# Preparing two tiles ahead of weight conversions, early loads of float64 units, and zero fills behind the fifth tile

## The chip, the cores and the metric

The kernel runs on one core of one Trainium2 chip. The metric is the device time of one execution in microseconds; the figure of a kernel is the median over its runs. The trace is one further execution, taken by the hardware profiler. PE is TensorE (matmuls), PEld its weight loads, DVE VectorE, ACT ScalarE, POOL GpSimd, SP SyncE, which here only starts transfers. SPq, ACTq and POOLq are DMA starts by those engines.

## The reference

Three stages follow each other, cut here to what is computed:

```
for t in range(768):                                   # recurrent attention, 4 x 8 heads of 48
    state = alpha[:, :, t, :, None] * state + outer(k[:, :, t], v[:, :, t])
    y[:, :, t] = q[:, :, t] @ state
x = y as (3072 tokens, 384)

logits = x @ w_gate + modality_bias[modality_id]       # 8 experts, the best one is taken
e_idx = argmax(logits);  gate_w = softmax(logits)[e_idx]
for e in range(8):
    out[mask] = gate_w * (relu(x[mask] @ w1[e]) @ w2[e])   # w1: 384 x 1024, w2: 1024 x 384

h = out @ w_in                                         # float64 weights, 384 x 2048
result = (h * sigmoid(h)) @ w_out                      # float64 weights, 2048 x 384
```

The tokens' experts are known only when the attention has run, so which rows a tile of 128 tokens holds and which expert's weights it needs are values that the kernel computes and reads back into registers.

## The kernel before

**Order of the work.** `attention` handles 24 steps of 128 positions and sorts the tokens' rows by expert: each step's rows are scattered by POOL to a table XS in DRAM, at a place that their expert and rank give. After 16 steps the most frequent expert is known, and its first 256 rows are taken as two early tiles, whose two expert products run in float32 at the end of `attention` (`early`). After step 24 a chain of small DVE operations (`table`) writes `tabi`, the list of the remaining tiles: expert, first row, and whether the expert's weights must be loaded anew. `main` then works through these tiles (slots 0, 1, 2, ...; `slot32` for the first three, in float32, `slot` for the others, in pairs of float16 numbers) and, in between, through chunks of 256 finished tokens of the last stage: `into` is the product with `w_in`, `outof` that with `w_out`. The beginning is slot 0, slot 1, `into` of chunk 0, slot 2, `outof` of chunk 0. With the early tiles counted, slot 2 is the fifth tile.

**A slot.** `fetch` (SP) reads 128 rows of XS to `xr`; ACT scales them by the gate's weight; PE transposes them to `u_p` in PSUM; ACT copies these to `xg`, the operand of the first product. `weights` (SP) loads an expert's four pieces of 768 KB to `raw` 0 to 3 (0 and 1 hold w1, 2 and 3 w2). The first product (`h_p`) needs `raw` 0 and 1 and `xg`, the second (`yT_p`) `raw` 2 and 3. At the end `keep_ids` stores the rows' token numbers with a matmul to `id_p` and a DVE copy to `idrow`.

**The float64 weights.** They come as 32 units of 384 words for each partition (0 to 15 of `w_in`, 16 to 31 of `w_out`). `unit_load` starts the transfer of 384 KB to one of two buffers `uraw`; `unit_conv` makes a float32 word in `wf` out of it on DVE (one TENSOR_SCALAR, two SCALAR_TENSOR_TENSOR), ACT rounds that to float16 (`wih`, `woh`), and DVE computes the rest (`wil`, `wol`). A buffer's next load stands behind its conversion. Units 0 to 8 (`CONV_A = 9`) are converted in `attention`'s plan, the others in `main`'s.

**Who sets the order.** Every operation is entered in a `Plan` with its engine, an estimated cost, what it reads and writes, and a priority (the smallest first). `Plan.run` lets an engine that falls free take the ready operation of the smallest priority, by estimated times, and writes out each engine's instructions in that order. On the chip each engine then works in this order, and waits on semaphores where an operand isn't there. `attention` and `main` are two plans: all of the first plan's instructions of an engine precede the second's. A plan knows nothing of what the other has left unfinished. In `main` PE is taken to be free from 2.0 us on (`PE0`). A key `seq` makes operations of one name follow each other in the order in which they are entered.

**Rows of XS.** Writes of rows are declared independent of each other (`apart`); a fetch waits for all writes of rows that have been written out before it (`behind`), and these include the eight zero fills of `zeros`, which write 128 empty rows behind each expert's last row.

Of the kernel before, what the change touches and what calls it, by code (L numbers as in the profile page):

```python
# [12 lines left out]
I32 = mybir.dt.int32  # L13
# [7 lines left out]
P = 128  # L21
B, H, S, D = 4, 8, 768, 48
NC = S // P
NSTEP = B * NC
NP = H // 2
DM = H * D
# [6 lines left out]
E = 8  # L33
# [171 lines left out]
class Kernel:  # L205
    def __init__(self, ctx, tc, qka, al0, v, vT, mod, gate, mbias, w1, w2, wi, wo, out):
        self.ctx, self.tc, self.nc = ctx, tc, tc.nc
        nc = tc.nc
        self.PE, self.ACT, self.DVE, self.POOL, self.SP = nc.tensor, nc.scalar, nc.vector, nc.gpsimd, nc.sync
        self.qka, self.al0, self.v, self.vT = qka, al0, v, vT  # L210
        self.mod, self.gate, self.mbias = mod, gate, mbias
        self.w1, self.w2, self.wi, self.wo, self.out = w1, w2, wi, wo, out

        self.rows = []
        const = self.pool(ctx, "const")
        keep = self.pool(ctx, "keep")
        dram = self.pool(ctx, "dram", space=DRAM)
        self.XS = dram.tile([E * CAP + P, ROW], F32, name="XS")

        self.wih = keep.tile([P, NF2, KD, P], F16, name="wih")  # L220
        self.wil = keep.tile([P, NF2, KD, P], F16, name="wil")
        self.raw = [keep.tile([P, 4 * DM], F32, name=f"raw{j}") for j in range(4)]
        self.uraw = [keep.tile([P, 2 * UNIT], I32, name=f"uraw{j}") for j in range(2)]
        self.wf = [keep.tile([P, UNIT], I32, name=f"wf{j}") for j in range(2)]
        self.yT0 = [keep.tile([P, KD, P * EARLY], F16, name=f"yT0{s}") for s in "hl"]
        self.xr = [keep.tile([P, ROW], F32, name=f"xr{j}") for j in range(3)]
        self.idc = [keep.tile([P, 1], I32, name=f"idc{j}") for j in range(4)]

        self.ident = const.tile([P, P], F32, name="ident")
        self.ident16 = const.tile([P, P], F16, name="ident16")  # L230
        self.w128 = const.tile([P, 1], F16, name="w128")
        self.ones16 = const.tile([P, P], F16, name="ones16")
        self.before16 = const.tile([P, P], F16, name="before16")
        self.rev = const.tile([P, E], F32, name="rev")
        self.ebase = const.tile([P, E], F32, name="ebase")
        self.pid = const.tile([P, 1], F32, name="pid")
        self.tabi = const.tile([P, 5], I32, name="tabi")
        self.cum = const.tile([P, E], F16, name="cum")
        self.star = const.tile([P, E], F32, name="star")
        self.endf = const.tile([P, E], F32, name="endf")  # L240
        self.endi = const.tile([P, E], I32, name="endi")
        self.pick = const.tile([P, 1 + EARLY], I32, name="pick")
# [27 lines left out]
        self.DVE.tensor_tensor(out=out, in0=in0, in1=in1, op=op)  # L270


    def unit_load(self, pl, u, prio, after=()):
        raw = self.uraw[u % 2]
        src = self.wi if u < NUNIT else self.wo
        c = UNIT * (u % NUNIT)
        pl.op("ACT", 0.4, lambda: self.ACT.dma_start(out=raw, in_=src[:, c:c + UNIT].bitcast(I32)),
              r=after, w=[("uraw", u % 2)], prio=prio, dma=1.1)

    def unit_conv(self, pl, u, prio):  # L280
        raw = self.uraw[u % 2].rearrange("p (a b) -> p a b", b=2)
        hw, lw = raw[:, :, 1], raw[:, :, 0]
        w = self.wf[u % 2]
        wf = w.bitcast(F32)
        hi, lo = (self.wih, self.wil) if u < NUNIT else (self.woh, self.wol)
        fl = (lambda t: t.rearrange("p a b c -> p (a b c)")) if u < NUNIT else flat
        c = UNIT * (u % NUNIT)
        hv, lv = fl(hi)[:, c:c + UNIT], fl(lo)[:, c:c + UNIT]
        s = 16.0 if u < NUNIT else 32.0
        kr, kw, ko = ("uraw", u % 2), ("wf", u % 2), ("w2nd", u)  # L290
        pl.op("DVE", c_dve(UNIT, fast=True), lambda: self.DVE.tensor_scalar(
            out=w, in0=hw, scalar1=3, scalar2=0x3FFFFFFF,
            op0=ALU.logical_shift_left, op1=ALU.bitwise_and), r=[kr], w=[kw], prio=prio)
        pl.op("DVE", c_dve(UNIT), lambda: self.stt(w, hw, -0x40000000, w, ALU.bitwise_and, ALU.bitwise_or),
              r=[kr], w=[kw], prio=prio)
        pl.op("DVE", c_dve(UNIT), lambda: self.stt(w, lw, 29, w, ALU.logical_shift_right, ALU.bitwise_or),
              r=[kr], w=[kw], prio=prio)
        pl.op("ACT", c_act(UNIT), lambda: self.act(hv, wf, scale=s), r=[kw], w=[ko], prio=prio)
        pl.op("DVE", c_dve(UNIT), lambda: self.stt(lv, wf, s, hv, ALU.mult, ALU.subtract), r=[kw], w=[ko], prio=prio)
# [14 lines left out]
    def attention(self, ctx):  # L314
# [372 lines left out]
        for i in range(NSTEP):  # L687
            if i + 2 < NSTEP:
                prep(i + 2)
            if i + 4 < NSTEP:  # L690
                load(i + 4)
            chunk(i)
            if i == EARLY_AT:
                for a in range(EARLY):
                    self.fetch(pl, None, i + 1.5, a)
                self.weights(pl, None, PICK + 2)
        for u in range(CONV_A):
            self.unit_conv(pl, u, 100 + u)
            if u + 2 < 2 * NUNIT:
                self.unit_load(pl, u + 2, 100 + u)  # L700


        def view(key, off, n, shape, dt=F32):
# [12 lines left out]
                      ("y_p", d) if d < 2 else "A0") for d in range(KD)]  # L716
        vt = float(NSTEP) + 2
        self.early(pl, vt)
        self.weights(pl, 0, NSTEP + 1)
        self.fetch(pl, 0, NSTEP + 2)  # L720
        self.fetch(pl, 1, NSTEP + 2)
        pl.run()

    def choose_early(self, pl, a1, tot_p, pr):
# [24 lines left out]

        pl.op("DVE", 0.2, ends, r=["tot_p", "dc"], w=["ends"], prio=pr + 2)  # L750

    def zeros(self, pl, prio):

        def fill(e):
            row = self.POOL.value_load(self.endi[0:1, e:e + 1], min_val=e * CAP, max_val=e * CAP + NT)
            self.apart(self.POOL.dma_start(out=self.XS[ds(row, P), :], in_=self.XS[E * CAP:E * CAP + P, :]))

        for e in range(E):
            pl.op("POOL", 1.1, lambda e=e: fill(e), r=["zero"], w=[("XS", NSTEP + e)], prio=prio + 0.1 * e, dma=0.6)

    def table(self, pl, a1, tot_p, pr):

# [79 lines left out]
    def fetch(self, pl, t, prio, early=None):  # L842
        n = self.ring_of(t, early)
        xr, kxr = self.xr[n], ("xr", n)

        def get():
            row = self.val(self.SP, t, 1, 0, E * CAP) if t is not None else self.SP.value_load(
                self.pick[0:1, 1 + early:2 + early], min_val=0, max_val=E * CAP)
            self.behind(self.SP.dma_start(out=xr, in_=self.XS[ds(row, P), :]))

        pl.op("SP", 1.1, get, r=["tab" if t is not None else "pick"] + [
            ("XS", i) for i in (range(PICK) if t is None else range(NSTEP) if t < FULL else range(NSTEP + E + 1))], w=[kxr], prio=prio, dma=0.6)

    def weights(self, pl, t, prio):
        SP = self.SP
# [35 lines left out]
    def main(self, ctx):  # L891
# [25 lines left out]
        for w in ORDER:  # L917
            if w == "i":
                vt = self.chunk_in(pl, 0, vt)
            elif w == "o":  # L920
                vt = self.chunk_out(pl, 0, vt)
            else:
                t += 1
                vt = self.step(pl, t, vt)
            if t == 1 and w == "s":
                self.zeros(pl, vt)
                for u in range(CONV_A, 2 * NUNIT):
                    pr = CV0 + CV1 * (u - NUNIT)
                    self.unit_conv(pl, u, pr)
                    if u + 2 < 2 * NUNIT:  # L930
                        self.unit_load(pl, u + 2, pr)
        for c in range(1, NCHUNK - 2):
            assert all(self.spot(u)[0] > 2 * c + 1 for u in range(t + 1, NSLOT))
            vt = self.chunk_in(pl, c, vt)
# [43 lines left out]
    def keep_ids(self, pl, t, xr, kxr, kyp, vt):  # L978
# [1 line left out]
        lo, hi = self.spot(t)  # L980
        pl.op("PE", 0.07, lambda: self.mm(self.id_p[0:2, :P], xr.bitcast(F16)[:, 2 * DM:2 * DM + 2], self.ident16, True, True),
              r=[kxr, kyp], w=["id_p"], prio=vt + 7)
        pl.op("DVE", 0.3, lambda: self.DVE.tensor_copy(out=self.idrow[:, ds(self.place(self.DVE, t), P)], in_=self.id_p[0:2, :P]),
              r=["id_p"], w=[("TC", b) for b in range(lo, hi + 1)], prio=vt + 9)

    def slot32(self, pl, t, vt):

        act, mm = self.act, self.mm
        n = self.ring_of(t, None)
        xr, kxr = self.xr[n], ("xr", n)  # L990
        xT, kxT = self.xg[t % 2].bitcast(F32).rearrange("p (a b) -> p a b", b=P), ("xg", t % 2)
        tp, ktp = self.u_p[t % 2][:, :DM].rearrange("p (a b) -> p a b", b=P), ("u_p", t % 2)
        y_p, kyp = self.y_p[0].rearrange("p (a b) -> p a b", b=P), ("yT_p", 0)
        pl.op("ACT", c_act(DM) + 0.05, lambda: act(xr[:, :DM], xr[:, :DM], scale=xr[:, DM + 1:DM + 2]), w=[kxr], prio=vt - GV)

        def transp():
            for k in range(KD):
                self.PE.transpose(out=tp[:, k], in_=xr[:, P * k:P * k + P], identity=self.ident)

        pl.op("PE", 0.34, transp, r=[kxr], w=[ktp], prio=vt - GV, work=0.3)  # L1000
        pl.op("ACT", c_act(DM, True) + 0.05, lambda: act(xT, tp), r=[ktp], w=[kxT], prio=vt - GV)
        for half in range(2):
            w = self.raw[half].rearrange("p (k f) -> p k f", k=KD)
            hp, khp = self.h_p[half].rearrange("p (a b) -> p a b", b=P), ("h_p", half)
# [275 lines left out]
```

## Time and profile before

| | us |
|---|---|
| median of 3 runs | 776.24 (775.47 to 777.59) |
| profiled execution, its own time | 776.01 |
| its span in the trace | 774.2 |
| PE busy | 748.4 |
| DVE busy | 514.5 |
| ACT busy | 397.7 |

The profiled execution's own time is 1.8 us more than its span: what lies around the span isn't in the trace. Busy time is that of instructions at work; a DMA start counts on no engine. Matmuls are pipelined, so their durations overlap, and a stretch is read from start to start. In a timeline the columns are start, duration (of a whole run of like instructions, "x" tells how many), engine, line, operation, output and inputs, and in brackets the engine's idle time before it with what ended that.

### The profile page before, as it was taken

What the parts mean: (1) busy time and instruction counts of PE and PEld (TensorE: products, weight loads), DVE (VectorE), ACT (ScalarE), POOL (GpSimd) and SP (SyncE); (2) the same over time, 40 slices, a digit from 0 to 9 for tenths busy, and PEclk for the clock granted to TensorE, in tenths of its full rate; (3) what the DMA queues carried; (4) which work ended last, traced back from release to release, by engine and by line L of the source; (5) the groups of instructions that cost most, each with busy time, mean ns of one, the idle gap of its engine ahead of it and who ended that gap; (6) DMA issues with size and microseconds to landing.
All of it is one profiled execution on the core that took longest, in us unless ns stands there. A gap on an engine that the chain in (4) does not pass through costs nothing. (4 is left out here: it accounts for less than half of the span.)

```text
span 774.2 us, 18772 instructions
## 1 busy us (share of the span) xinstructions
PE 748.4 (97%) x7751; PEld 628.3 (81%) x7751; DVE 514.5 (66%) x847; ACT 397.7 (51%) x659; POOL 113.6 (15%) x152
## 2 busy tenths in 40 slices
PE   8999999984999999999999999999999999999996
PEld 4999898874988879879799698798896987977683
DVE  6999999955699946728477477397473883723250
ACT  4776757622356536636366375376462861613140
POOL 3345747602000101010000000000100000000000
PEclk9999999995999999999999999999999999999999
DMA  8876869386545111000034120110100553000000
GB/s 291 287 249 219 281 217 381 120 298 191 155 119 135 36 29 43 23 23 21 22 95 132 23 43 22 31 33 23 43 12 12 162 124 128 12 2 24 1 22 20
DMA packets 42027, 79.39 MB, mean 103 GB/s; under 512 B 19792, under 2 KB 29648, under 8 KB 41808
## 3 DMA queue, kind: packets, MB, share of 16 engines
q1 hardware_dynamic: 34000, 54.27, 22.7%
q10 hardware_dynamic: 4608, 12.58, 5.6%
q0 software_dynamic: 3328, 11.28, 3.9%
q8 instruction: 62, 1.02, 0.5%
q14 instruction: 29, 0.24, 0.1%
HBM read 124.12 MB, written 11.48 MB: 175 GB/s over the span
## 5 line engine op out<-in xcount | busy, mean ns | idle before, releaser
L264 PEld LDWEIGHTS <-pch 128*128 128x128 f16 x1920 | 149.2, 98 | 2.3
L267 DVE SCALAR_TENSOR_TENSOR pcl<-raw,pch 128x1536 f16<-128x1536 f32 x80 | 138.6, 1752 | 16.0 <-ACT pch L261 16.0
L264 PE MATMUL u_p<-yTh,wih 128*128 128x256 f16 x528 | 144.0, 273 | 1.1 <-PEq L949 1.1
L264 PE MATMUL u_p<-yTh,wil 128*128 128x256 f16 x528 | 143.9, 273 | 0.0
L264 PE MATMUL u_p<-yTl,wih 128*128 128x256 f16 x528 | 143.9, 273 | 0.0
L264 PE MATMUL o_p<-woh,gh 128*128 128x384 f16 x384 | 125.3, 326 | 0.0
L264 PE MATMUL o_p<-wol,gh 128*128 128x384 f16 x384 | 125.2, 326 | 0.0
L264 PE MATMUL o_p<-woh,gl 128*128 128x384 f16 x384 | 125.2, 326 | 0.0
L264 PEld LDWEIGHTS <-wih 128*128 128x128 f16 x1152 | 111.1, 98 | 15.1 <-issue 1.4
L261 ACT ACTIVATE pch<-raw 128x1536 f16<-128x1536 f32 x80 | 117.6, 1478 | 1.8 <-PE yT_p L264 1.8
L264 PEld LDWEIGHTS <-gh 128*128 128x128 f16 x768 | 73.8, 98 | 47.7
L1200 POOL DMA_INDIRECT out_dram<-osb,idc x24 | 27.0, 1127 | 551.2 <-DVE osb L1197 439.5
L264 PEld LDWEIGHTS <-pcl 128*128 128x128 f16 x960 | 93.9, 98 | 0.0
L267 DVE SCALAR_TENSOR_TENSOR gl<-g,gh 128x512 f16<-128x512 f32 x96 | 65.8, 689 | 33.2 <-ACT gh L261 32.9
L261 ACT ACTIVATE gh<-g 128x512 f16<-128x512 f32 x96 | 60.1, 629 | 48.7 <-DVE g L270 48.0
L264 PE MATMUL h_p<-xT,pch 128*128 128x128 f16 x960 | 84.4, 219 | 0.0
L264 PE MATMUL yT_p<-h,pch 128*128 128x128 f16 x960 | 83.8, 219 | 0.0
L264 PE MATMUL h_p<-xT,pcl 128*128 128x128 f16 x480 | 82.3, 219 | 0.0
L264 PE MATMUL yT_p<-h,pcl 128*128 128x128 f16 x480 | 82.0, 219 | 0.0
L1197 DVE TENSOR_SCALAR osb<-o_p 128x384 f32<-128x384 f32 x12 | 6.7, 558 | 111.7 <-PE o_p L264 111.7
L270 DVE TENSOR_TENSOR g<-u_p,sg 128x512 f32<-128x512 f32 x96 | 65.4, 685 | 16.7 <-ACT sg L261 16.3
L261 ACT ACTIVATE osb<-o_p 128x384 f32<-128x384 f32 x12 | 5.9, 490 | 136.2 <-PE o_p L264 136.2
(181 smaller groups left out, 1162.6 us busy)
## 6 DMA issues: line engine op xcount, KB each, us to landing
raw<-in_w_dram SPq DMA_DIRECT2D x94, 768.0 KB
reg<-in_qka_dram SPq DMA_DIRECT2D x23, 768.0 KB
uraw<-in_wi_dram ACTq DMA_DIRECT2D x16, 384.0 KB
uraw<-in_wo_dram ACTq DMA_DIRECT2D x16, 384.0 KB
v<-in_v_dram SPq DMA_DIRECT2D x24, 224.0 KB
xr<-XS SPq DMA_DIRECT2D x25, 200.0 KB
vT<-in_vT_dram SPq DMA_DIRECT2D x24, 192.0 KB
XS<-XS POOLq DMA_DIRECT2D x8, 200.0 KB, 3.2
```

What stands on the lines that cost most here:

```text
L261: self.ACT.activation(out=out, in_=in_, func=func, **k)
L264: self.PE.matmul(out=out, lhsT=lhsT, rhs=rhs, start=first, stop=last, skip_group_check=True)
L267: self.DVE.scalar_tensor_tensor(out=out, in0=in0, scalar=scalar, in1=in1, op0=op0, op1=op1)
L270: self.DVE.tensor_tensor(out=out, in0=in0, in1=in1, op=op)
L1197: lambda osb=osb, o_p=o_p: self.DVE.tensor_scalar(out=osb, in0=o_p, scalar1=1.0 / 65536, scalar2=None, op0=ALU.mult)),
L1200: pl.op("POOL", 1.04, lambda idc=idc, osb=osb: self.POOL.indirect_dma_start(out=self.out[:, :], out_offset=IOA(ap=idc[:, :], axis=0), in_= ...
```

## The change

Four edits. The scaling, transposing and copying of slots 0 and 1 get priority 30 below the slot's due time, where it was 3 (`g`). The fetches of slots 0 and 1 are entered ahead of slot 0's weights, with a priority one lower, and join the sequence `raw` of the weights, so that SP starts fetch 0, fetch 1, then `raw` 2, 3, 0, 1. The loads of units 4 to 8 go to five places of `reg`, the memory of the attention's inputs of steps 22 and 23 and of their decay values, in place of the two buffers; these loads and those of units 9 and 10 (to the two buffers) are started by SP at priorities 23.4 to 24.0, where ACT started them behind conversions. And `zeros` is entered behind slot 2 in place of slot 1, with a dependency on slot 2's copy to `idrow`. No arithmetic changes.

```diff
+    def unit_at(self, u):
+        n = u - 2 if 4 <= u < CONV_A else u % 2
+        return self.uraw[n], ("uraw", n)
+
     def unit_load(self, pl, u, prio, after=()):
-        raw = self.uraw[u % 2]
+        raw, kr = self.unit_at(u)
+        name, eng = ("SP", self.SP) if 4 <= u < CONV_A + 2 else ("ACT", self.ACT)
...
-        pl.op("ACT", 0.4, lambda: self.ACT.dma_start(out=raw, in_=src[:, c:c + UNIT].bitcast(I32)),
-              r=after, w=[("uraw", u % 2)], prio=prio, dma=1.1)
+        pl.op(name, 0.4, lambda: eng.dma_start(out=raw, in_=src[:, c:c + UNIT].bitcast(I32)),
+              r=after, w=[kr], prio=prio, dma=1.1)
...
+        for n in range(2, CONV_A - 2):
+            at = 22 + 6 * (n - 2)
+            self.uraw.append(part(at, 6, [6 * P], I32))
+            pl.spans["uraw", n] = [("r", at + b) for b in range(6)]
         for u in range(CONV_A):
             self.unit_conv(pl, u, 100 + u)
-            if u + 2 < 2 * NUNIT:
+            if u + 2 < 4:
                 self.unit_load(pl, u + 2, 100 + u)
+            for v in range(4, CONV_A + 2) if u == 3 else ():
+                self.unit_load(pl, v, NSTEP - 1 + 0.1 * v)
...
         self.early(pl, vt)
+        self.fetch(pl, 0, NSTEP + 1)
+        self.fetch(pl, 1, NSTEP + 1)
         self.weights(pl, 0, NSTEP + 1)
-        self.fetch(pl, 0, NSTEP + 2)
-        self.fetch(pl, 1, NSTEP + 2)
...
-    def zeros(self, pl, prio):
+    def zeros(self, pl, t, prio):
...
+            made = self.POOL.dma_start(out=self.XS[ds(row, P), :], in_=self.XS[E * CAP:E * CAP + P, :])
+            self.tc.add_manual_dep(made.ins, self.kept[t].ins.name, ...)
+            self.apart(made)
...
-            pl.op("POOL", 1.1, lambda e=e: fill(e), r=["zero"], w=[("XS", NSTEP + e)], ...)
+            pl.op("POOL", 1.1, lambda e=e: fill(e), r=[("TC", EARLY + t)], w=[("XS", NSTEP + e)], ...)
...
             ("XS", i) for i in ...], w=[kxr], prio=prio, dma=0.6,
+              seq="raw" if t in (0, 1) else None)
...
             if t == 1 and w == "s":
-                self.zeros(pl, vt)
                 for u in range(CONV_A, 2 * NUNIT):
...
+        self.zeros(pl, t, vt)
         for c in range(1, NCHUNK - 2):
...
     def slot32(self, pl, t, vt):
+        g = GV if t > 1 else 30
...
-        pl.op("ACT", c_act(DM) + 0.05, lambda: act(xr[:, :DM], ...), w=[kxr], prio=vt - GV)
+        pl.op("ACT", c_act(DM) + 0.05, lambda: act(xr[:, :DM], ...), w=[kxr], prio=vt - g)
...
-        pl.op("PE", 0.34, transp, r=[kxr], w=[ktp], prio=vt - GV, work=0.3)
-        pl.op("ACT", c_act(DM, True) + 0.05, lambda: act(xT, tp), r=[ktp], w=[kxT], prio=vt - GV)
+        pl.op("PE", 0.34, transp, r=[kxr], w=[ktp], prio=vt - g, work=0.3)
+        pl.op("ACT", c_act(DM, True) + 0.05, lambda: act(xT, tp), r=[ktp], w=[kxT], prio=vt - g)
```

## Rows read from the trace of the kernel before

**Rows 1.** The page: busy time of the engines over the span.
```profile
PE 748.4 (97%) x7751; PEld 628.3 (81%) x7751; DVE 514.5 (66%) x847; ACT 397.7 (51%) x659; POOL 113.6 (15%) x152
```
**Rows 2.** Windows of 5 us: busy times, granted clock, DMA share, GB/s.
```profile
165.00:170.00 5.00, 5.00 (x25) 4.41 (x24) 3.05 (x7) 0.91 (x2) 0.00 (x0) 1.00 1.02 416
170.00:175.00 5.00, 1.41 (x7) 0.90 (x5) 2.69 (x7) 0.80 (x2) 0.21 (x1) 0.90 0.70 249
```
**Rows 3.** Timeline of PE at the seam between the two plans.
```profile
167.79 3.62 PE L264 MATMUL A_p<-reg,eraw 128*128 128x256 f32 x16
178.42 1.54 PE L998 MATMUL u_p<-ident,xr 128*128 128x128 f32 x6 [7.01 <-DVE wil L267]
185.86 8.09 PE L264 MATMUL h_p<-xg,raw 128*128 128x128 f32 x48 [5.90 <-ACT xg L261]
...
199.38 5.62 PE L264 MATMUL h_p<-xg,raw 128*128 128x128 f32 x48
```
**Rows 4.** Timeline of ACT in the same stretch.
```profile
171.45 0.39 ACT L261 ACTIVATE yT0h<-A_p 128x256 f16<-128x256 f32 x1 [2.60 <-PE A_p L264]
...
177.31 0.52 ACT L261 ACTIVATE wih<-wf 128x384 f16<-128x384 f32 x1 [1.28 <-DVE wf L267]
...
177.75 1.12 ACT L261 ACTIVATE xr<-xr 128x384 f32<-128x384 f32 x2
183.86 0.52 ACT L261 ACTIVATE wih<-wf 128x384 f16<-128x384 f32 x1 [4.99 <-DVE wf L267]
...
184.39 0.49 ACTq L277 DMA_DIRECT2D uraw<-in_wi_dram  x1
185.31 0.87 ACT L261 ACTIVATE xg<-u_p 128x384 f32<-128x384 f32 x2 [0.46 <-DMA XS<-XS]
```
**Rows 5.** Timeline of DVE in the same stretch.
```profile
157.83 0.17 DVE L748 CAST endi<-endf 128x8 int32<-128x8 f32 x1
...
171.87 0.42 DVE L267 SCALAR_TENSOR_TENSOR yT0l<-A_p,yT0h 128x256 f16<-128x256 f32 x1 [1.11 <-ACT yT0h L261]
...
178.82 0.36 DVE L291 TENSOR_SCALAR wf<-uraw 128x384 int32<-128x384 int32 x1 [0.40 <-DMA uraw<-in_wi_dram]
182.06 0.36 DVE L291 TENSOR_SCALAR wf<-uraw 128x384 int32<-128x384 int32 x1 [2.88 <-DMA uraw<-in_wi_dram]
```
**Rows 6.** Timeline of SP's transfer starts in the same stretch.
```profile
159.19 1.65 SPq L867 DMA_DIRECT2D raw<-in_w_dram  x3
161.89 0.33 SPq L849 DMA_DIRECT2D xr<-XS  x1
162.63 0.33 SPq L867 DMA_DIRECT2D raw<-in_w_dram  x1
164.16 13.80 SPq L849 DMA_DIRECT2D xr<-XS  x2
```
**Rows 7.** Narrow windows at the fall and the rise of PE's clock (columns as in rows 2).
```profile
173.80:174.00 0.20, 0.00 (x0) 0.00 (x0) 0.07 (x1) 0.00 (x0) 0.00 (x0) 0.97 0.78 307
...
190.80:191.20 0.40, 0.40 (x4) 0.40 (x4) 0.00 (x0) 0.00 (x0) 0.00 (x0) 0.68 0.09 32
```
**Rows 8.** Timeline of DVE at the end of the attention: last decay value of step 23.
```profile
139.34 0.68 DVE L267 SCALAR_TENSOR_TENSOR kf<-reg 128x512 f32<-128x512 f32 x1
```
**Rows 9.** Timelines of ACT and PE: unit 29 and its first use.
```profile
250.90 0.52 ACT L261 ACTIVATE woh<-wf 128x384 f16<-128x384 f32 x1 [1.50 <-DVE wf L267]
...
261.00 0.33 PE L264 MATMUL o_p<-woh,gh 128*128 128x384 f16 x1
```
**Rows 10.** Timelines of POOL (zero fills), and of DVE, SP and ACT behind slot 2.
```profile
188.76 0.49 POOL L756 DMA_DIRECT2D XS<-XS  x1 [0.71 <-issue]
...
243.92 0.27 DVE L983 CAST idrow<-id_p 2x128 f16<-2x128 f32 x1
...
244.19 0.36 SPq L849 DMA_DIRECT2D xr<-XS  x1
...
247.93 1.47 ACT L261 ACTIVATE pch<-raw 128x1536 f16<-128x1536 f32 x1
```

More of the change, by code (lines that the diff above doesn't have):

```diff
@@ L212, in __init__ @@
         self.w1, self.w2, self.wi, self.wo, self.out = w1, w2, wi, wo, out
-        self.rows = []
+        self.rows, self.kept = [], {}
         const = self.pool(ctx, "const")
@@ L270, in tt @@
         self.DVE.tensor_tensor(out=out, in0=in0, in1=in1, op=op)
+    def unit_at(self, u):
+        n = u - 2 if 4 <= u < CONV_A else u % 2
+        return self.uraw[n], ("uraw", n)
     def unit_load(self, pl, u, prio, after=()):
-        raw = self.uraw[u % 2]
+        raw, kr = self.unit_at(u)
+        name, eng = ("SP", self.SP) if 4 <= u < CONV_A + 2 else ("ACT", self.ACT)
         src = self.wi if u < NUNIT else self.wo
         c = UNIT * (u % NUNIT)
-        pl.op("ACT", 0.4, lambda: self.ACT.dma_start(out=raw, in_=src[:, c:c + UNIT].bitcast(I32)),
-              r=after, w=[("uraw", u % 2)], prio=prio, dma=1.1)
+        pl.op(name, 0.4, lambda: eng.dma_start(out=raw, in_=src[:, c:c + UNIT].bitcast(I32)),
+              r=after, w=[kr], prio=prio, dma=1.1)
     def unit_conv(self, pl, u, prio):
-        raw = self.uraw[u % 2].rearrange("p (a b) -> p a b", b=2)
+        raw, kr = self.unit_at(u)
+        raw = raw.rearrange("p (a b) -> p a b", b=2)
         hw, lw = raw[:, :, 1], raw[:, :, 0]
@@ L289, in unit_conv @@
         s = 16.0 if u < NUNIT else 32.0
-        kr, kw, ko = ("uraw", u % 2), ("wf", u % 2), ("w2nd", u)
+        kw, ko = ("wf", u % 2), ("w2nd", u)
         pl.op("DVE", c_dve(UNIT, fast=True), lambda: self.DVE.tensor_scalar(
@@ L750, in blank @@
         pl.op("DVE", 0.2, ends, r=["tot_p", "dc"], w=["ends"], prio=pr + 2)
-    def zeros(self, pl, prio):
+    def zeros(self, pl, t, prio):
         def fill(e):
             row = self.POOL.value_load(self.endi[0:1, e:e + 1], min_val=e * CAP, max_val=e * CAP + NT)
-            self.apart(self.POOL.dma_start(out=self.XS[ds(row, P), :], in_=self.XS[E * CAP:E * CAP + P, :]))
+            made = self.POOL.dma_start(out=self.XS[ds(row, P), :], in_=self.XS[E * CAP:E * CAP + P, :])
+            self.tc.add_manual_dep(made.ins, self.kept[t].ins.name, mybir.DependencyInfo(
+                mybir.DependencyClass.Sync, mybir.DependencyReason.DATA), reason="not among the first transfers")
+            self.apart(made)
         for e in range(E):
-            pl.op("POOL", 1.1, lambda e=e: fill(e), r=["zero"], w=[("XS", NSTEP + e)], prio=prio + 0.1 * e, dma=0.6)
+            pl.op("POOL", 1.1, lambda e=e: fill(e), r=[("TC", EARLY + t)], w=[("XS", NSTEP + e)], prio=prio + 0.1 * e, dma=0.6)
     def table(self, pl, a1, tot_p, pr):
@@ L851, in fetch @@
         pl.op("SP", 1.1, get, r=["tab" if t is not None else "pick"] + [
-            ("XS", i) for i in (range(PICK) if t is None else range(NSTEP) if t < FULL else range(NSTEP + E + 1))], w=[kxr], prio=prio, dma=0.6)
+            ("XS", i) for i in (range(PICK) if t is None else range(NSTEP) if t < FULL else range(NSTEP + E + 1))], w=[kxr], prio=prio, dma=0.6,
+              seq="raw" if t in (0, 1) else None)
     def weights(self, pl, t, prio):
@@ L982, in keep_ids, with keep @@
               r=[kxr, kyp], w=["id_p"], prio=vt + 7)
-        pl.op("DVE", 0.3, lambda: self.DVE.tensor_copy(out=self.idrow[:, ds(self.place(self.DVE, t), P)], in_=self.id_p[0:2, :P]),
-              r=["id_p"], w=[("TC", b) for b in range(lo, hi + 1)], prio=vt + 9)
+        def keep():
+            self.kept[t] = self.DVE.tensor_copy(out=self.idrow[:, ds(self.place(self.DVE, t), P)], in_=self.id_p[0:2, :P])
+        pl.op("DVE", 0.3, keep, r=["id_p"], w=[("TC", b) for b in range(lo, hi + 1)], prio=vt + 9)
     def slot32(self, pl, t, vt):
         act, mm = self.act, self.mm
+        g = GV if t > 1 else 30
         n = self.ring_of(t, None)
@@ L993, in slot32 @@
         y_p, kyp = self.y_p[0].rearrange("p (a b) -> p a b", b=P), ("yT_p", 0)
-        pl.op("ACT", c_act(DM) + 0.05, lambda: act(xr[:, :DM], xr[:, :DM], scale=xr[:, DM + 1:DM + 2]), w=[kxr], prio=vt - GV)
+        pl.op("ACT", c_act(DM) + 0.05, lambda: act(xr[:, :DM], xr[:, :DM], scale=xr[:, DM + 1:DM + 2]), w=[kxr], prio=vt - g)
         def transp():
```

## The prediction

> **What bounds the kernel now.** The page comes first: PE is busy 97% of the span, DVE 66%, ACT 51% [rows 1]. That share is no proof that PE sets every stage, so the windows come next. PE is busy 5.00 of 5.00 us up to 170, and then falls to 1.41 of 5 at the seam between the two plans [rows 2]. The timeline of PE there shows what is missing. The last early product ends at 167.79 + 3.62 = 171.41. Then 7.01 us pass idle, six transposes run until 179.96, 5.90 us pass idle again, and slot 0's first product starts at 185.86 [rows 3]. Between 171.41 and 185.86 there are 14.45 us in which PE does only the transposes. Nothing later looks like it: slot 0's and slot 1's products follow each other, and the windows behind them are full. What PE gains at this seam is gained at the end, as long as nothing behind it falls short.
>
> The price has a second part. The granted clock falls from 1.00 to half (2.4 to 1.2 GHz) at about 174.0, 2.6 us into the idle stretch, and comes back at about 191.1 [rows 7]. Slot 0's first product therefore takes 8.09 us where slot 1's takes 5.62: 2.47 us [rows 3].
>
> Why PE waits is seen on ACT. Its first plan ends with the conversion of unit 8 at 177.31, and only then, at 177.75, does it scale slot 0's rows; the transposes start at 178.42, behind the first of these two. The copies that release the product come at 185.31, behind the rounding of unit 9 (183.86), that of unit 10, and a load at 184.39 [rows 4]. DVE shows what was late: the conversions of units 9 and 10 begin at 178.82 and 182.06, each as its transfer lands [rows 5]. So both gaps are waits for float64 units, in front of work that doesn't need them; ACT takes its instructions in the written order. (PE's wait for DVE's `wil` in the first gap is a coincidence of times; the scaled rows end at the same moment.)
>
> **The change, part by part.**
>
> *Loads of units 4 to 8.* Their places are free when step 23's last decay value is done, at 139.34 + 0.68 = 140.0 [rows 8]. Five transfers of 384 KB are 1.97 MB, 4.7 us at 416 GB/s [rows 2]; even at half that rate they are in by 150. So DVE, free of the table at 158.0 [rows 5], converts units 3 to 8 without waiting for transfers. One unit is a TENSOR_SCALAR and three SCALAR_TENSOR_TENSOR; I take 1.9 us for it: the way from unit 10's first operation to unit 9's rounding, 182.06 to 183.86, is 1.8 us and holds one and four such operations less overlap [rows 4, 5]. Five and a half units are 10.5 us, with the three `yT0l` of 0.42 us 11.7: to 169.7. DVE's first plan then ends with the last `yT0l`, 171.87 + 0.42 = 172.29 [rows 5], which PE's early product sets. The moved loads cost SP five starts of 0.33 us [rows 6], hidden, since SP starts nothing else between the early fetches and 159; if they delayed the early fetches the price would be up to 2 us. I take 0.
>
> *ACT's first plan* ends with the last `yT0h`, 171.45 + 0.39 = 171.84 [rows 4]. The fetches, now ahead of the weights, start at about 159 to 161 instead of 161.89 and 164.16 [rows 6], and are not what ACT waits for. Scaling slot 0: 0.62 (half of the pair's 1.12, and the overlap), to 172.5. Three transposes: at most 0.77, half of 1.54 at the low clock, to 173.2 [rows 3, 4].
>
> *The new priority* does less than its 30 says. I follow the second plan's estimates by hand. ACT scales both tiles from 0 to 0.93. PE is free at 2.0, so slot 0's transposes end at 2.34 and their copy is ready at 2.54. DVE takes units 9 and 10 from 0 on, alternating, and unit 9's rounding is ready at 2.09. ACT is idle then and takes it, and at 2.5 the load of unit 11; only at 2.9 does it find the copy, with the smallest priority. So unit 9 and one load stay ahead of slot 0's copy, and unit 10 and the second load go behind both copies. On the chip DVE starts unit 9 at 172.29: 0.36 for its first operation, then the 1.8 us read above, gives the rounding at 174.5. From there to the copy it was 1.45 us with two roundings and two loads [rows 4]; without a rounding of 0.5 and a load of 0.5, 0.5 to 1.0: 175.0 to 175.5. From copy to product 185.31 to 185.86, 0.55 [rows 3, 4]. Slot 0's first product starts at 175.5 to 176.1; I take 175.9.
>
> *The weights of slot 0* are started later: SP now does two fetches first, each about 1.1 us with its register (161.89 less the end of three starts at 160.84) [rows 6], so `raw` 1 starts at some 164.5 instead of 162.63. What must land by 176: `raw`, 3.15 MB, two fetches of 128 rows of 1600 B, 0.41 MB, units 9 and 10, 0.79 MB: 4.35 MB, 10.5 us at 416 GB/s [rows 2] from about 160, to 170.5 to 173. Hidden, with 3 us of cover. The Trainium skill speaks against any gain from the change of engine as such: "DMA: Bandwidth & Descriptors", section "Issuing engines are not separate DMA queues", says that transfers started by several engines run on the same 16 DMA engines and interleave, and that spreading them only saves the time of starting them. By that rule the move to SP buys nothing and the earlier start everything; the sum above, which counts all bytes against one rate, is the same with it.
>
> *Zero fills* leave the stretch at 174 to 190 for one behind slot 2, where POOL has only the chunk's output to start. Taken at 0; the rival below prices it.
>
> *What comes behind.* Everything else on PE moves up together, but some units must be there earlier. Among the groups of `outof` that I compared, the closest is unit 29's: rounded at 250.90 + 0.52 with its rest half a us later, used at 261.00 [rows 9], 9 us of slack. Were no conversion any earlier, a gain of 10 would cost about 1 there; but unit 11's load follows unit 9's rounding, which moves up by 9. I take 0.
>
> **The sum.** 185.86 − 175.9 = 9.96 us, if the clock is low as before when the product starts. 776.01 − 9.96 = 766.05 us. The profiled execution is 0.23 under the median of the runs, which is within their spread: 766 for both.
>
> **The rivals.**
>
> *The clock stays up* (763.5). The idle stretch behind the transposes is 175.9 − 173.6 = 2.3 us, against 2.6 before the fall [rows 7], and about 1 us of transposes lies ahead of it. If it doesn't fall, the 2.47 us come on top. For it: the gap is shorter. Against: the whole stretch from 171.4 on is 4.5 us with little in it. I can't decide that from the trace.
>
> *The preparation does go ahead of everything* (761). If ACT copies slot 0 before unit 9: 173.2 + 0.49 (the copy) makes a product at 173.7, 12.2 us, and with the clock up 14.6: 761.4. It needs other estimates in the plan than those I followed.
>
> *Transfers are late* (768 to 771). If units 9 and 10 come behind the weights on SP, unit 10 lands at about 174 and unit 9's rounding slips to 176: product at 177.7, 767.9. If the weights keep pace with neither fetches nor units, the first product waits for `raw` 1; with the rate of 249 GB/s [rows 2] for half of the bytes the burst ends at 175 to 179: up to 769, and with a delayed early fetch 771. For it: in the burst the DMA engines are full (1.02) [rows 2].
>
> *A new wait behind slot 2 takes it back* (775 to 778). The fills now follow slot 2's copy to `idrow` (243.92); slot 5's fetch follows slot 2 as well (244.19) [rows 10]. If the plan writes the fetch out behind the fills, SP holds it until all eight have landed: eight at a pitch of 1.20 [rows 10] are 9.6 us, and their landing on top. SP's next starts, the weights of slot 4, stand behind it, and ACT's conversion of these (247.93), in front of evictions that PE needs: up to 10 to 12 us. It decides from the point where the fetch is entered behind the last fills. Against it: the fetch needs only slot 2's `id_p` matmul, the fills also the copy behind it, so the fetch should come first.
>
> **How the numbers follow.** Forecast 0.5 (own range 764.7 to 767.5), clock up 0.2, all ahead 0.08, transfers late 0.15, the new wait 0.07. The range 762 to 770.5 leaves out the new wait, most of the third case and the top of the fourth. 0.3% of 776 is 2.3 us, about what a measurement of this kernel can tell from no change: the new wait falls half within it and half above, so faster 0.93, same 0.04, slower 0.03.
>
> **What would show it.** On ACT after: `yT0h`, scaling, one rounding of a unit, one load, then both copies, at about 175; the second rounding behind them. On DVE no wait for a `uraw` transfer between 158 and 174. PE's first gap near 1 us and its second near 2.5, the product at 175.9 with a duration of 8.1 (low clock) or 5.6. SP: fetches ahead of `raw`. No idle PE between slot 2 and slot 5. I would be wrong if ACT's first plan still ended with a late unit, if DVE stood in its written order behind a `yT0l` that is late, or if PE showed a wait for `raw`.

## The result and the profile after

The changed kernel takes 766.33 us, the median of 4 runs (765.99 to 767.87), the kernel before on the same chip 776.48 (775.47 to 777.59). The ratio is 0.9873, its 95% interval 0.9853 to 0.9892. The prediction was 766.0, its range 762 to 770.5.

The profiled execution is the slowest of these four: 767.87, with a span of 766.2. Its busy times, on the page, answer to [rows 1]; the engines do what they did.

```profile
PE 747.5 (98%) x7751; PEld 627.4 (82%) x7751; DVE 512.5 (67%) x847; ACT 397.3 (52%) x659; POOL 112.9 (15%) x152
```

The timeline of PE at the seam, after, answers to [rows 3]:

```profile
169.46 3.62 PE L264 MATMUL A_p<-reg,eraw 128*128 128x256 f32 x16
174.21 0.89 PE L1018 MATMUL u_p<-ident,xr 128*128 128x128 f32 x6 [1.14 <-DVE wf L298]
177.40 8.16 PE L264 MATMUL h_p<-xg,raw 128*128 128x128 f32 x48 [2.29 <-ACT xg L261]
...
190.99 5.62 PE L264 MATMUL h_p<-xg,raw 128*128 128x128 f32 x48
```

The early product ends at 169.46 + 3.62 = 173.08, and slot 0's first product starts at 177.40: 4.32 us, where it was 14.45. Two idle stretches remain, 1.14 and 2.29 us. The first ends with the scaling of slot 0's rows (the row names DVE, which has a unit's operation at the same moment; in experiments 5 to 8 the same wait is put down to ACT's `xr`). The second one is still ended by ACT's copy.

The timeline of ACT, after, answers to [rows 4]:

```profile
173.11 0.38 ACT L261 ACTIVATE yT0h<-A_p 128x256 f16<-128x256 f32 x1 [3.07 <-PE A_p L264]
173.39 1.11 ACT L261 ACTIVATE xr<-xr 128x384 f32<-128x384 f32 x2
175.93 0.52 ACT L261 ACTIVATE wih<-wf 128x384 f16<-128x384 f32 x1 [1.43 <-DVE wf L267]
175.93 0.33 ACTq L283 DMA_DIRECT2D uraw<-in_wi_dram  x1
176.85 0.49 ACT L261 ACTIVATE xg<-u_p 128x384 f32<-128x384 f32 x1 [0.40 <-ACT wih L261]
...
177.61 0.52 ACT L261 ACTIVATE wih<-wf 128x384 f16<-128x384 f32 x1
```

The last conversion of the first plan is gone from in front of the scaling. One rounding (unit 9, at 175.93) and one load stand in front of slot 0's copy; unit 10's rounding (177.61) stands behind both copies. The transposes had been ready since 174.21 + 0.89 = 175.10; the copy came at 176.85. So the new priority does not put the preparation ahead of all conversions: one is left, and it still sets the start.

DVE's timeline, after, answers to [rows 5]:

```profile
159.38 0.17 DVE L761 CAST endi<-endf 128x8 int32<-128x8 f32 x1
159.47 0.55 DVE L267 SCALAR_TENSOR_TENSOR wf<-uraw,wf 128x384 int32<-128x384 int32 x1
...
173.53 0.42 DVE L267 SCALAR_TENSOR_TENSOR yT0l<-A_p,yT0h 128x256 f16<-128x256 f32 x1 [3.03 <-ACT yT0h L261]
173.87 0.62 DVE L298 TENSOR_SCALAR wf<-uraw 128x384 int32<-128x384 int32 x2
174.40 1.96 DVE L267 SCALAR_TENSOR_TENSOR wf<-uraw,wf 128x384 int32<-128x384 int32 x4
```

Conversions follow the table at once, and DVE has 3.03 us to spare in front of the last `yT0l`. Both units 9 and 10 are there when they are wanted (173.87, no wait), where DVE waited for their transfers until 178.82 and 182.06. SP's timeline, after, answers to [rows 6]:

```profile
161.43 1.58 SPq L865 DMA_DIRECT2D xr<-XS  x2
164.82 2.34 SPq L884 DMA_DIRECT2D raw<-in_w_dram  x4
168.03 0.33 SPq L865 DMA_DIRECT2D xr<-XS  x1
```

Two fetches stand ahead of the weights, and slot 2's fetch (168.03) starts some ten us earlier than before (the last of two from 164.16 on for 13.80). Windows of 5 us, after, have the columns of [rows 2]:

```profile
170.00:175.00 5.00, 3.87 (x21) 2.98 (x19) 1.90 (x6) 1.43 (x4) 0.00 (x0) 1.00 0.93 381
175.00:180.00 5.00, 2.71 (x13) 2.61 (x13) 3.25 (x7) 2.31 (x5) 0.00 (x0) 0.59 0.52 153
180.00:185.00 5.00, 5.00 (x35) 5.00 (x35) 2.65 (x6) 1.01 (x2) 0.00 (x0) 0.73 0.21 47
```

The clock falls here too (0.59, 0.73), and slot 0's product takes 8.16 us, 2.54 more than slot 1's.

**The account.** The gap gives 14.45 − 4.32 = 10.13 us. Slot 0's product costs 0.07 more than before. The early product ends 1.67 us later in this execution, and 0.39 is lost behind slot 0 (by the span's end less the start of slot 0's second product: 774.2 − 193.78 before, 766.2 − 185.39 after); 0.3 of that is one longer wait of PE's sequencer, 1.4 us against 1.1. 10.13 − 0.07 − 1.67 − 0.39 = 8.00, the difference of the spans. The medians differ by 10.15: the other three runs of the changed kernel, 765.99 to 766.60, are 1.3 to 1.9 us under the profiled one.

The later early product is a matter of three waits for ACT inside attention, at 119.10, 130.16 and 159.86. The groups of PE's waits from 100 to 172, after (us in total, how many, the longest):

```profile
PE st_b L264 <- ACT ktok L261: 1.0, 2, 0.6
PE kt_p L264 <- ACT reg L261: 0.4, 1, 0.4
```

They are 1.4 of the 1.67 us, and the kernel before has none of them. The experiments show that the early loads don't bring them: they come and go with one and the same kernel (last section).

### The profile page after: what moved, and what is told of

Same layout as the page of the kernel before. It is cut to its first block, busy times and chain, and to the rows that moved or that the text cites. A ratio compares the mean times of both kernels' runs of the same rounds, so it can differ in the third digit from the quotient of the medians.

```text
span 766.2 us, 18784 instructions
## 1 busy us (share of the span) xinstructions
PE 747.5 (98%) x7751; PEld 627.4 (82%) x7751; DVE 512.5 (67%) x847; ACT 397.3 (52%) x659; POOL 112.9 (15%) x152
## 5 line engine op out<-in xcount | busy, mean ns | idle before, releaser
L261 ACT ACTIVATE sg<-u_p 128x512 f32<-128x512 f32 x96 | 57.1, 594 | 37.4 <-PE u_p L264 37.2
```

Of the source, the lines that this page charges most:

```text
L261: self.ACT.activation(out=out, in_=in_, func=func, **k)
```

## The experiments

The theory is the prediction's: late float64 units in ACT's and DVE's written order make the gap, so the early loads carry the gain; the priority saves one rounding and one load; the order of the fetches and the zero fills are worth nothing. The main rivals were that the priority carries it, that the fetches do, and that the fills do. Experiments 1 to 4 ran on one chip, 5 to 8 on a second, 9 to 11 on a third, and 12 later on that third one; each ratio is against the kernel before on the same chip. A gap is the time from the early product's end to the start of slot 0's first product, read from the experiment's own rows.

**1. The loads alone,** put into the kernel before:

```diff
+        name, eng = ("SP", self.SP) if 4 <= u < CONV_A + 2 else ("ACT", self.ACT)
...
+            at = 22 + 6 * (n - 2)
+            self.uraw.append(part(at, 6, [6 * P], I32))
...
+            for v in range(4, CONV_A + 2) if u == 3 else ():
+                self.unit_load(pl, v, NSTEP - 1 + 0.1 * v)
```

> The kernel before with the early loads alone (units 4 to 8 into the attention's room, 4 to 10 started by SP). Theory A, conversions: PE waits at the seam because ACT and DVE have float64 units with late transfers in front of slot 0's preparation, so these loads alone bring most of the gain. Units 9 and 10 and two loads still stand ahead of slot 0's copies on ACT, which costs about 1 us against the full change: 767 to 768. Theory B, transfers: the gain comes from the fetches ahead of the weights and the fills out of the way, so the loads alone bring little: 773 to 776.

Measured: 766.83 (766.06 to 768.88) against 775.03, ratio 0.9900 (0.9875 to 0.9926). Timelines of PE, then of ACT, in this kernel:

```profile
167.41 3.62 PE L264 MATMUL A_p<-reg,eraw 128*128 128x256 f32 x16
172.16 1.09 PE L1011 MATMUL u_p<-ident,xr 128*128 128x128 f32 x6 [1.14 <-DVE wf L298]
176.28 8.46 PE L264 MATMUL h_p<-xg,raw 128*128 128x128 f32 x48 [3.03 <-ACT xg L261]
```

```profile
174.35 0.52 ACT L261 ACTIVATE wih<-wf 128x384 f16<-128x384 f32 x1
174.36 0.88 ACTq L283 DMA_DIRECT2D uraw<-in_wi_dram  x1
175.74 0.87 ACT L261 ACTIVATE xg<-u_p 128x384 f32<-128x384 f32 x2 [0.87 <-DMA XS<-XS]
178.93 0.62 ACT L261 ACTIVATE xr<-xr 128x384 f32<-128x384 f32 x1 [2.32 <-DMA xr<-XS]
```

The gap is 5.25 us. Two roundings (the second at 174.35) and two loads stand in front of the copies. The loads alone give nine tenths of the gap's gain (9.20 of 10.13).

**2. The priority alone:**

```diff
+        g = GV if t > 1 else 30
...
-        pl.op("ACT", c_act(DM, True) + 0.05, lambda: act(xT, tp), r=[ktp], w=[kxT], prio=vt - GV)
+        pl.op("ACT", c_act(DM, True) + 0.05, lambda: act(xT, tp), r=[ktp], w=[kxT], prio=vt - g)
```

> The kernel before with the lower priority number of slots 0 and 1 alone. Theory A: ACT's first plan still ends with unit 8 at about 177, and unit 9's rounding stays ahead of the copies, which DVE reaches only when unit 10's transfer has landed; the copies pass unit 10 alone, at most 1 us: 775 to 776.5, same as before. A rival, that the priority is what moves slot 0 ahead of the conversions, would give 766 to 770.

Measured: 773.70 (772.88 to 778.93) against 775.03, ratio 0.9987 (0.9954 to 1.0019), no difference that can be told, though under the 775 to 776.5 that were expected. PE's timeline:

```profile
177.60 1.54 PE L999 MATMUL u_p<-ident,xr 128*128 128x128 f32 x6 [6.51 <-DVE wil L267]
183.73 7.52 PE L264 MATMUL h_p<-xg,raw 128*128 128x128 f32 x48 [4.58 <-ACT xg L261]
```

Both waits stand; the gap is 183.73 − 171.10 = 12.63, 1.82 less than before. Unit 8 belongs to the first plan, which no priority of the second can pass, and unit 9 is still in front of the copy.

**3. All but the loads:** the changed kernel with `unit_load`'s lines and the five places as before (the first diff, reversed).

> The changed kernel with the early loads undone (all units through the two buffers, started by ACT), the other three edits kept. Theory A: most of the gain is lost, 773.5 to 776. Theory B (fetches and fills): the gain stays, 766 to 768.

Measured: 774.22 (773.22 to 777.97), ratio 0.9997 (0.9978 to 1.0016). Without the loads no gain can be told: the transposes start at 178.59 and the product at 183.90, a gap of 183.90 − 171.16 = 12.74.

**4. All but the fills:** `zeros` again behind slot 1, and without its dependency on `idrow`.

```diff
             if t == 1 and w == "s":
+                self.zeros(pl, vt)
...
-        self.zeros(pl, t, vt)
```

> The changed kernel with the zero fills back behind slot 1, the other three edits kept. Theory A: the fills run beside the weights' transfers between 165 and 185 and nothing on PE's way waits for them while the weights have 3 us of cover: 766 to 767. Theory B: the fills (200 KB read and written eight times) delay the weights of slot 0 or unit 11: 768 to 771, with a wait of PE for raw in the trace.

Measured: 765.44 (764.55 to 766.48), ratio 0.9883 (0.9862 to 0.9905), where the changed kernel has 0.9873. The gap is 175.18 − 170.87 = 4.31, as with the fills moved: by itself the move is worth nothing that can be told.

**5. All but the fetches' order:**

```diff
-        self.fetch(pl, 0, NSTEP + 1)
-        self.fetch(pl, 1, NSTEP + 1)
         self.weights(pl, 0, NSTEP + 1)
+        self.fetch(pl, 0, NSTEP + 2)
+        self.fetch(pl, 1, NSTEP + 2)
...
-              seq="raw" if t in (0, 1) else None)
```

> The changed kernel with the fetches of slots 0 and 1 back behind the weights on SP, the other three edits kept. Theory A: the rows still land before ACT has finished its first plan at about 171, as they did with the loads alone, so nothing waits: 765.5 to 767. Theory B: the rows land at the end of the burst, ACT's scaling waits to 173 or 174: 768 to 769.

Measured: 765.51 (764.89 to 766.37), ratio 0.9868 (0.9852 to 0.9884). The gap is 176.34 − 172.00 = 4.34. By itself the order of the fetches is worth nothing that can be told either.

**6. The copies ahead of unit 9.** By the prediction's reading of the plan, slot 0's copy loses to unit 9 because PE is taken to be free only at 2.0 us. This kernel is the changed one with

```diff
-PE0 = 2.0
+PE0 = 0.0
```

> The changed kernel with PE taken to be free at 0 in the second plan's estimates (2.0 in the changed kernel). The plan then writes both copies of slots 0 and 1 ahead of unit 9's rounding on ACT. Theory A: slot 0's first product no longer waits for unit 9's conversion and starts 2.2 us earlier (two copies and the load of unit 11 aside): 763.5 to 764.5, and some 761.5 if the shorter gap also keeps the clock up. Rival: the weights in raw 0 and 1 have not landed by then, and the product waits for them: 765.5 to 766.5, with a wait for raw in the trace.

Measured: 761.37 (760.35 to 767.76), ratio 0.9830 (0.9802 to 0.9858). PE's timeline, ACT's, and a window of 5 us:

```profile
166.90 3.62 PE L264 MATMUL A_p<-reg,eraw 128*128 128x256 f32 x16
171.65 0.89 PE L1018 MATMUL u_p<-ident,xr 128*128 128x128 f32 x6 [1.14 <-ACT xr L261]
172.80 5.62 PE L264 MATMUL h_p<-xg,raw 128*128 128x128 f32 x48 [0.26 <-ACT xg L261]
```

```profile
172.26 0.87 ACT L261 ACTIVATE xg<-u_p 128x384 f32<-128x384 f32 x2 [0.31 <-PE u_p L1018]
173.37 0.53 ACT L261 ACTIVATE wih<-wf 128x384 f16<-128x384 f32 x1 [0.24 <-DVE wf L267]
```

```profile
170.00:175.00 5.00, 3.61 (x28) 2.93 (x27) 3.86 (x9) 3.76 (x8) 0.00 (x0) 1.00 0.53 188
```

The copies go first, the gap is 2.28, and the product takes 5.62: the clock stays at 1.00. Against the profile of the changed kernel that is 2.04 of the gap and 2.54 of the product; against 9, whose product takes 7.25, it is 2.04 and 1.63. This is the prediction's rival of the preparation ahead of everything, which it put at 761.4; it needs one more edit than the change made.

**7. PE kept busy.** The changed kernel, with 36 matmuls behind slot 1's transposes whose product nobody uses:

```diff
+        if t == 1:
+            def keep_busy():
+                for _ in range(36):
+                    mm(self.id_p[:, 256:384], self.ones16, self.before16, True, True)
+
+            pl.op("PE", 0.01, keep_busy, r=[ktp], w=["busy"], prio=vt - g)
```

> The changed kernel with 36 matmuls of 128 columns whose product is not used, on PE between slot 1's transposes and slot 0's first product, where PE is idle for 2.3 us. Theory A: the clock falls at the seam because PE idles, so it stays up now and slot 0's first product takes 5.6 us instead of 7.3 to 8.5: 763.5 to 764.7. Rival: the clock falls for the stretch as a whole, with the wait ahead of the transposes, or the added matmuls run over and delay the product: 766 to 767.

Measured: 763.38 (762.87 to 764.49), ratio 0.9840 (0.9827 to 0.9853). PE's timeline:

```profile
174.19 2.17 PE L264 MATMUL id_p<-before,ones 128*128 128x128 f16 x36
176.65 5.62 PE L264 MATMUL h_p<-xg,raw 128*128 128x128 f32 x48 [0.28 <-ACT xg L261]
```

The product starts 4.32 us behind the early product (168.71 + 3.62), as after the change, but takes 5.62. So it is PE's idling in the second wait that makes the product slow here: with work in it, even useless work, the product is fast, and the first wait of 1.14 us is still there.

**8. Both:** experiment 6 with 18 such matmuls.

> The two before together: copies ahead of unit 9 and 18 unused matmuls in the gap that is left. Theory A: the two gains add up, 2.2 and 1.7 to 2.6 us: 761.3 to 762.5. Rival: with the shorter gap the clock stays up by itself, so that the matmuls add nothing to the run with the copies first: the same time as that run.

Measured: 762.14 (761.71 to 762.44), ratio 0.9825 (0.9812 to 0.9838). The product takes 5.58, the gap is 173.71 − 170.84 = 2.87. Nothing is added to experiment 6: there the clock stayed up over the gap of 2.28 us, with the transposes in it, without any help.

**9. The changed kernel once more,** unaltered, on the third chip, as the measure for 10 and 11.

> The changed kernel once more, unaltered, on the chip of the next two runs. Theory A takes its profiled execution's late early product (173.1 where all the others have 170.5 to 172.0) for one execution's ACT stall and not for a cost of the change: the early product ends at 170.5 to 172.0 here, and the median is 765 to 766.5. Rival: the moved loads delay the attention by 1 to 2 us in every execution: it ends near 173 again.

Measured: 767.99 (766.74 to 770.98) against 776.38, ratio 0.9889 (0.9871 to 0.9908). The gap is 181.44 − 177.12 = 4.32 again and the product 7.25. The median lies above the 765 to 766.5 that were expected, and what was expected of the early product's end missed by 5 us: it ends at 177.12. A window at the start of attention shows the larger part of that:

```profile
15.00:20.00 5.00, 5.00 (x38) 4.72 (x38) 4.83 (x13) 1.84 (x6) 0.00 (x0) 0.54 0.98 368
```

PE ran at about half clock between 15 and 25 (0.50 in the window from 20), where every profile of experiments 1 to 8 shows 1.00, and it waited three times for ACT, 1.7 us in all, as in the profile of the changed kernel above and in none of 1 to 8, six of which have the early loads. Experiment 12, with the same three waits and a clock of 1.00 there, has the early product's end at 174.05, so the half clock makes some 3 us. The last section comes back to both.

Why is the product faster here, 7.25 against 8.16? Windows at the seam in this profile:

```profile
180.00:185.00 5.00, 3.56 (x22) 3.56 (x23) 3.17 (x7) 2.28 (x5) 0.00 (x0) 0.77 0.50 157
185.00:190.00 5.00, 5.00 (x42) 5.00 (x42) 2.01 (x5) 2.02 (x4) 0.00 (x0) 0.89 0.32 88
```

With 1.00 up to 180, the shares 0.77 and 0.89 put the half clock from 182.7 to 186.1: the fall came 1.3 us after the product had started, and 3.4 us of it ran slow. After the change, 0.59 and 0.73 in its windows put it from 175.9 to 182.7: the fall came 1.5 us ahead of the product, and 5.3 us of it ran slow. The products lose 1.63 and 2.54 against 5.62, near half of the time at half clock in both.

**10. Loads, priority and copies first, without the new fetch order and fills:** the kernel before with the edits of 1, 2 and 6.

> The kernel before with the early loads, the new priority, and PE taken as free at 0 in the second plan; fetches and fills as before. Theory A: only the conversions' transfers and ACT's written order matter, so this is as fast as the changed kernel with the copies first: 761 to 762.5. Rival: with the product at 173 the fetches behind the weights, or the fills beside them, come too late, and it gives back 2 us or more: 763.5 to 766.

Measured: 767.52 (766.74 to 771.42), ratio 0.9885 (0.9866 to 0.9903). The expectation of 761 to 762.5 missed. The rival held in its cause: once the copies go first, the fetches and the fills do matter. The time lies above the rival's 763.5 to 766 too, on a chip on which the changed kernel itself takes 767.99. SP's timeline, POOL's and ACT's:

```profile
170.36 12.28 SPq L862 DMA_DIRECT2D xr<-XS  x3
```

```profile
179.51 0.57 POOL L769 DMA_DIRECT2D XS<-XS  x1 [17.03 <-DVE wf L298]
```

```profile
185.78 0.61 ACT L261 ACTIVATE xr<-xr 128x384 f32<-128x384 f32 x1 [4.07 <-DMA xr<-XS]
...
186.30 1.06 ACT L261 ACTIVATE h<-h_p 128x512 f32<-128x512 f32 x2
```

The gap is as in 6 (2.28, product 5.62). But slot 2's fetch, the third of SP's run, starts only at about 182.3, behind the first fill, and ACT waits 4.07 us for its rows, in front of both copies of slot 0's `h`. PE's waits follow (groups of waits from 175 on):

```profile
PE u_p L264 <- DVE g L270: 1.3, 2, 1.1
PE yT_p L264 <- ACT h L261: 1.1, 1, 1.1
```

From slot 0's product to the span's end it is 769.8 − 180.15 = 589.65 here, and 762.7 − 176.33 = 586.37 in experiment 12 on the same chip: 3.28 us are lost. The two groups are 2.4 of these; 12 has 0.2 of the first and none of the second. The medians of the two differ by 3.07. Experiment 1 has the same late fetch and an ACT wait of 2.32, but there slot 0's product runs at the low clock and needs nothing from ACT in that time. And either edit alone keeps the fetch ahead: in 4, with the fills as before, SP starts it at 170.08 and the first fill follows at 174.15; in 5, with the fetches as before, it starts at about 166.4 and the fills are behind slot 2. That is why 4 and 5 each show nothing.

**11. Priority and copies first alone:** the kernel before with the edits of 2 and 6.

> The kernel before with the new priority and PE taken as free at 0, without the early loads. Theory A: the first gap stays, since ACT's first plan still ends with unit 8 at 177; the second gap goes, since the copies no longer stand behind units 9 and 10: the product at about 179.7 with a low clock, 6 us earlier than before, 769 to 771. Rival: the product waits for something else once the copies are free (weights, zero fills, unit 9's transfer on another engine): 773 to 776.

Measured: 773.02 (770.73 to 778.50), ratio 0.9962 (0.9940 to 0.9983). PE's timeline:

```profile
180.74 1.54 PE L999 MATMUL u_p<-ident,xr 128*128 128x128 f32 x6 [6.89 <-DVE wil L267]
182.34 7.00 PE L264 MATMUL h_p<-xg,raw 128*128 128x128 f32 x48
...
211.63 0.27 PE L264 MATMUL u_p<-yT0h,wih 128*128 128x256 f16 x1 [1.69 <-DVE g L270]
```

and DVE's in front of that wait:

```profile
209.43 0.36 DVE L291 TENSOR_SCALAR wf<-uraw 128x384 int32<-128x384 int32 x1 [2.11 <-DMA uraw<-in_wo_dram]
...
210.90 0.69 DVE L270 TENSOR_TENSOR g<-u_p,sg 128x512 f32<-128x512 f32 x1
```

The gap is 182.34 − 173.85 = 8.49, as expected: the second wait is gone, the first stands. But of these 6.0 us about 2.6 are given back behind slot 0 (772.2 − 189.18 = 583.02 from slot 0's second product to the end, 774.2 − 193.78 = 580.42 before), 1.69 of it at the wait shown. DVE waited 2.11 us for a unit's transfer there, and the `g` that PE needs stood behind that unit. So a unit that is late anyway turned up again later, when only the order was changed. The expected 769 to 771 was some 2 us too low.

**12. Experiment 6 once more,** unaltered, on the chip of 9 to 11.

> The changed kernel with the copies first once more, unaltered, since the run with the loads and the order alone came out 6 us slower, on another chip. If fetches and fills matter once the copies go first, this one keeps its ratio to the kernel before, 0.980 to 0.986, about 761 to 764, and ACT's scaling of slot 2's rows doesn't wait for their transfer. Rival: the 6 us were the chip's, and the ratio here varies as much, 0.986 to 0.990, 765 to 768.

Measured: 764.45 (763.41 to 764.97) against 777.51, ratio 0.9822 (0.9797 to 0.9847), as in 6 (0.9830). PE's timeline and ACT's:

```profile
170.43 3.62 PE L264 MATMUL A_p<-reg,eraw 128*128 128x256 f32 x16
...
176.33 5.62 PE L264 MATMUL h_p<-xg,raw 128*128 128x128 f32 x48 [0.26 <-ACT xg L261]
```

```profile
177.80 0.60 ACT L261 ACTIVATE xr<-xr 128x384 f32<-128x384 f32 x1
```

The gap is 2.28 and the product 5.62; slot 2's scaling (177.80) waits for nothing. So the loss in 10 comes from the edits it leaves out, not from the chip. With 8, which can't be told from it, this is the fastest version of the study, below the changed kernel by 0.004 to 0.007 of the time, and the intervals of 9 and 12, on one chip, do not touch.

## Why the prediction was right

- **What bounds the seam** was read rightly: two waits for float64 units in front of work that doesn't need them. The loads alone close most of it (1); all the rest without them gives nothing that can be told (3).
- **The loads' cost** was taken as 0, at most 2 if they delayed the early fetches. In 1, 4 and 5 the early product ends at 171.03, 170.87 and 172.00, before at 171.41 [rows 3]; they cost nothing that shows.
- **The order on ACT** came out as worked through by hand: one rounding and one load ahead of the copies, the other rounding behind. From the early product's end to slot 0's product the prediction had 175.9 − 171.41 = 4.49, measured 4.32. The six transposes of both slots took 0.89, so slot 0's three about half a us, where at most 0.77 was said; the way from the rounding's start to the copy 0.92 where 0.5 to 1.0 was.
- **The clock** was taken low, with 0.2 for the other case. It was low: 8.16 and 7.25 us in two executions of the changed kernel, 8.09 before. The prediction couldn't decide this from the trace, and the runs do for this kernel: with 1.14 us idle, the transposes and 2.29 us idle the clock fell (after, 9), with 1.14 and 0.26 it stayed up (6, 12), and with the second wait filled it stayed up too (7).
- **The priority** was said to do less than its 30 says. It saves one rounding and one load once the loads are early: 0.9 us of the gap between 1 and the changed kernel, and 1.4 between the medians of 1 and 4, whose intervals overlap (these differ by the order of the fetches too).
- **Fetches and fills at nothing** is right for the change as it was made (4, 5). It was argued by bytes and by POOL's free time, and that was incomplete: what the two edits do is to keep slot 2's fetch ahead of the fills. One of them is enough, the low clock hides it without either (1), and the two together are worth some 3 us once the product is fast (10 against 12; one of them alone was not tried there).
- **The transfers** were on time. PE shows no wait for `raw`, not even in 6, where the product starts 2 us sooner behind the early product; DVE shows none for a unit of the seam. By the rule that the prediction took from the Trainium skill ("DMA: Bandwidth & Descriptors", section "Issuing engines are not separate DMA queues") only the earlier start counts, not the engine; no run here moves the one without the other.
- **The new wait behind slot 2** did not come. Slot 5's fetch starts at 235.80 and the first of the moved fills at 239.00: the fetch went ahead, for the reason given. PE is busy 25.00 of 25 us in both windows from 200 to 250.
- **The sum** took 9.96 for the gap, measured 10.13 in the profile, and 10.15 between the medians. The profiled execution itself gained only 8.14: the early product ended 1.67 later, for which the waits for ACT account but for 0.3, and what comes behind, taken at 0, cost 0.39. That the median of 766.33 lies so close to 766.0 is therefore partly luck: the low clock's price moved by 0.9 us between executions, and on the third chip the same kernel gained 8.39 (9). DVE left the table at 159.55 instead of 158.0, 1 us of it with the later attention, and still had 3 us to spare.

## What to carry to other kernels

When a schedule is written out from estimates, look at what stands in front of the late instruction in its engine's order, and why the plan put it there: here one constant, the time at which the second plan takes PE to be free, was worth 3.7 to 4.6 us between traces, and 3.5 between the medians of 9 and 12, on top of the ten that the four edits gave. An edit that measures nothing alone may be the cover for the next one: test such edits together, and again after the bottleneck in front of them has moved. A short idle stretch on PE costs more than its length if the clock falls in it or just behind it, so read the duration of the next product beside the gap.

## What the runs showed of the hardware that was not expected

- The price of the low clock differs between executions: the same 48 matmuls took 7.00 to 8.46 us at seams with the clock fallen, and 5.58 or 5.62 with it up. In the two profiles of the changed kernel the difference is how much of the product fell into the half clock, 5.3 or 3.4 us (experiment 9). The Trainium skill ("TensorE: Matmul & The Clock Gate", section "What's actually happening") says of the start of a kernel that the number of matmuls at the low clock varies from run to run; 8.16 and 7.25 us for the changed kernel's product agree with that, at a later place.
- In two executions (9 and 10) PE ran at about half clock for the windows from 15 to 25, long before the seam; in 7 and 11 the window from 10 to 15 has 0.66. Those of 9 and 10 were the slowest of their kernels' runs, by 2.7 and 3.5 us over the next. What set it off is open.
- The three waits for ACT in attention stand in the profiles of the changed kernel and of 9 to 12, and in none of the kernel before and of 1 to 8. In the same five profiles ACT is idle for 3.8 to 4.6 us in front of its copy of `kt_p`, and the trace puts the end of that on something outside the core; in the others the same copy waits 2.10 us for PE. Experiment 11 shows it without the early loads and 1 and 4 to 8 don't with them, so the loads are not the cause. Experiment 12 shows it and 6, the same kernel, doesn't. Two of the three waits lie before that copy, so its delay can't be what makes them. Experiments 9 to 12 ran on one chip, 1 to 8 on two others, so it may go with the chip; that is a guess, and what ACT waits for stays open.
